# A longer ring for the converted w_in, partly in the place of the second batch's x, and a new set of planner shifts

## The chip, the core and the metric

The kernel runs on one core of a Trainium2 chip. The metric is the device time of one execution in microseconds (us), as the median of several runs. A profiled execution gives the trace that the rows below come from. Engines: PE is the matrix engine (TensorE, PEld its weight loads), DVE is VectorE, ACT is ScalarE, POOL is GpSimd, SP is the queue from which all transfers are issued.

## What is computed

Three stages on 4 batches of 576 tokens, 8 heads of 64, model width 512, in float32 accuracy:

```python
# attention with a decaying causal bias, b = 4, h = 8, s = 576, d = 64
scores = q @ k.T / 8 + min(bias(cumsum(relu(s))), 0), causal
x = softmax(scores) @ v                     # (2304, 512) after joining the heads
h = x @ w_in                                # w_in: 512 x 2048
x2 = (h * cos(h)) @ w_out                   # w_out: 2048 x 512
y = max(x2 @ w1, x2 @ w2, x2 @ w3) @ wo2    # 512 x 768 each, and 768 x 512
```

The weights of the second and third stage come as 64-bit floats.

## The kernel before

**Order of the work.** The kernel is written as a list of operations, each with an engine (or a choice of engines), an estimated duration, a key, and the pieces of memory that it reads and writes. A planner (`Plan`, L45 to L245) works out from the order in the list who must wait for whom, and then lays the operations out in time: each engine takes, of the operations that are ready by the planner's estimates, the one with the smallest key. The order per engine that comes out is fixed in the program. An operation with a choice of engines is offered to the later ones in its list only after a delay (`FLEX`, us by engine). The keys are a step number times 3 plus a shift from tables: `Q_AT`, `K_AT`, `V_AT` for the loads and conversions of q, k and v, `W_AT` for w_in, `S_AT`, `Z_AT`, `T_AT` for the scores, the products with v and the transposes of a step, `O_AT` for w_out. Where the plan leaves PE idle in the first 150 us, it is given matmuls on a constant tile whose result nobody reads (L1538, "fillers" below), and after that none.

**Attention** goes in 32 steps `st`: for each batch b, two ranges r of queries (256 and 320), four pairs p of heads. A step makes its scores (PE, L718 and L722), takes minimum and exponential (DVE L731, ACT L737), splits the weights into two float16 halves (ACT or POOL L412/L416, DVE L442), turns them by a DMA transpose (L754), multiplies with v (PE, L784, all steps in bank 4) and writes x as two float16 halves (ACT L797, DVE L802).

**w_in** comes in 16 chunks of 512 KB through two raw buffers. A chunk c is put from 64 bits into float32 by three DVE operations (L459, L462, L465), into a buffer of the ring `win_b`; its maximum is found on ACT (L477). When four chunks (a group) are there, their common power of two is made (DVE, and PE at L501), and the four are split into float16 halves: `hi` on ACT (L412), or for the fourth on POOL first (L416), and `lo` on DVE (L442) or POOL (L427). Only then can `mm1` (PE, L933) use them. The key of chunk c is `19.5 + 0.29 * c + W_AT[c]`, that of the group's split is the key of its last chunk. `mm1(t)` multiplies the x of a block t (a batch and a range, four steps) with all 16 chunks.

**Where things lie.** `wo_b` is the place of the later w_out, 16 buffers of 2 KB per partition, and is free for other things before:

```python
rb = wo_b[j]                                        # v of the first batch, piece j = 0..4 (L814)
vraw_b = wo_b[5:10]                                 # v of the other batches
win_b = wo_b[0:5] + [wo_b[10]] + stage_b            # ring of 8 for the converted w_in
x_other = [Buf(nc, wo_b[11].lo, 4096).ring(NPAIR),  # x of the second batch: steps 8 to 11 in
           Buf(nc, wo_b[13].lo, 5120).ring(NPAIR)]  # wo_b[11:13], steps 12 to 15 in wo_b[13:16]
value, sp = value_of(words, 512, rb.span(), take("win", win_b), key)     # chunk c (L1049)
```

So chunks 0 to 4 go into the buffers that hold pieces 0 to 4 of the first batch's v, and each can be written only when its piece has been split (`v_split`, L890). The order in which DVE, ACT, POOL and PE then work is in the tables alone.

**After attention** come the gate with `mm` by w_out (PE L1293), and the third stage in seven-product form (PE L1433, L1345); w_out is converted during the last steps of attention.

Of the kernel before, what the change touches and what calls it, by code (L numbers as in the profile page):

```python
# [287 lines left out]
def u_keys(i):  # L288
    return min(128 * (i + 1), S)
# [6 lines left out]
def dve1(n):  # L296
    return 0.07 + 0.00104 * n
# [35 lines left out]
def attn_moe_kernel(ctx, tc, qT, kT, v, s, w_in, w_out, w1, w2, w3, wo2, out):  # L333
# [11 lines left out]
    def alloc(size):  # L345
        b = Buf(nc, used[0], size)
        used[0] += size
        assert used[0] <= ARENA, used[0]
        return b
# [4 lines left out]
    def bspan(i, n=1):  # L354
        return ("ps", Plan.CELL * i, Plan.CELL * (i + n))
# [5 lines left out]
    stage_b = alloc(4096).ring(2)  # L361
    wo_b = alloc(NC1 * 2048).ring(NC1)
# [28 lines left out]
    dip_b = alloc(256)  # L391
    att1 = used[0]
    vraw_b = wo_b[5:10]
    win_b = wo_b[0:5] + [wo_b[10]] + stage_b
    pp_b = pp_b + raw_o
    x_other = [Buf(nc, wo_b[11].lo, 4096).ring(NPAIR), Buf(nc, wo_b[13].lo, 5120).ring(NPAIR)]
    x_last = [Buf(nc, v_b[4].lo, 4096).ring(NPAIR), Buf(nc, k_ring[1][0].lo, 5120).ring(NPAIR)]
# [5 lines left out]
    def take(name, ring):  # L403
        n = rings.get(name, 0)
        rings[name] = n + 1
        return ring[n % len(ring)]


    def scaled(out, src, by, key, cols, reads, writes, on="ACT DVE POOL", late=None, par=False):
# [9 lines left out]
        names = on.split()  # L419
        return P.flex(key, [(e, every[e][0], every[e][1], (FLEX[e] if late is None else late) * (i > 0)) for i, e in enumerate(names)],  # L420
                      reads, writes)

    def minus(out, a, b, key, cols, reads, writes, on="POOL DVE", late=None):
# [6 lines left out]
        names = on.split()  # L430
        return P.flex(key, [(e, every[e][0], every[e][1], (FLEX[e] if late is None else late) * (i > 0)) for i, e in enumerate(names)],
                      reads, writes)
# [47 lines left out]
    def weight_load(src, cols, raw, key, after=(), late=0):  # L480
        m = load(raw.ap(I64, cols), src, 1024 * cols + late, key, writes=[raw.span(0, 8 * cols)])
        P.after(m, [rows_out, *after])
        return raw.ap(I64, cols).bitcast(I32).rearrange("p (n two) -> p n two", two=2)
# [125 lines left out]
    def load_q(st, key):  # L609
        b, r, p = STEPS[st]  # L610
        q0, n = ((0, 256), (256, 384))[r]
        hb, lb = take("q", q_ring)
        hs, ls = [hb.span(0, 4 * n)], [lb.span(0, 4 * n)]
        raw = lb.ap(F32, n)
        load(raw, qT[b, p, :, q0:q0 + n], 512 * n, key - LEAD, writes=ls)
        if b == 0:
            q_of[st] = (raw, None, ls)
            return
        hi, lo = hb.ap(F32R, n), lb.ap(F32R, n)
        scaled(hi, raw, 1.0, key, n, ls, hs, on=Q_ON)  # L620
        minus(lo, raw, r_(hi), key + 0.2, n, ls + hs, ls, on=QS_ON)
        q_of[st] = (hi, lo, hs + ls)

    def load_k(b, p, key):
        hb, lb, rb = take("k", k_ring)
        hs, ls, rs = ([z.span()] for z in (hb, lb, rb))
        raw = lb.ap(F32, S)
        load(raw, kT[b, p], 295e3, key - LEAD, writes=ls, issue=0.65)
        if b == 0 and p == 0:
            row = rb.ap(F32, S)  # L630
            for c0, c1 in ((0, 320), (320, S)):
                first_row(c0, c1, row, [rb.span(4 * c0, 4 * (c1 - c0))], -30 if c0 == 0 else F2_KEY)
            ones = one_b.ap(F32, 128)
            bias = [(ones[64 * h:64 * h + 64], row[64 * h:64 * h + 64]) for h in range(2)]
            bias.append((onef_b.ap(F32, 128), row))
            rs = [rb.span(), one_b.span(), onef_b.span()]
        else:
            row, ones = rb.ap(F32R, S), oner_b.ap(F32R, 128)
            gb = take("got", got_b)
            got, gs = gb.ap(F32, S), [gb.span()]  # L640
            for h in range(2):
                load(got[64 * h:64 * h + 2], rows_dram[b * H + 2 * p + h], 4608, key - RLEAD,
                     reads=[dspan("rows"), dspan("rows", 1)], writes=gs)
            scaled(row, got, 1.0, key, S, gs, rs, on=K_ON)
# [19 lines left out]
    def attention(st):  # L664
# [11 lines left out]
        for i in units:  # L676
            n = u_keys(i)
            tg = 3 * st + i - units[0] + S_AT[st]
            a = 128 * (i - units[0])
# [81 lines left out]
        for j in range(nj):  # L761
# [27 lines left out]

            P.add("PE", 0.05 + 0.16 * max(nu, 0) + 0.1 * r + 0.25 * (j == 0), 3 * st + 2 + Z_AT[st], values,  # L790
                  reads=[ptb.span(), v_of[b, j][1].span()], writes=[bspan(4)])
# [7 lines left out]
            ("DVE", dve1(nq), lambda: nc.vector.tensor_scalar(  # L799
                out=xh, in0=xps, scalar1=us, scalar2=None, op0=ALU.mult), FLEX["DVE"])],  # L800
            reads=[bspan(4)], writes=xh_s)
# [100 lines left out]
    def evac(out, src, key, cols, reads, writes, by=None, on="ACT DVE"):  # L902
# [5 lines left out]
        }  # L908
        P.flex(key, [(e, every[e][0], every[e][1], FLEX[e] * (i > 0)) for i, e in enumerate(on.split())],
               reads, writes)  # L910
# [38 lines left out]
    def out_weights():  # L949
        ws = ws_b.ap(F32, NC1)  # L950
        for c in range(NC1):
            key = WO_KEY + c + O_AT[c]
            rb = take("ro", raw_all)
# [63 lines left out]
    for p in range(NPAIR):  # L1017
        load_k(0, p, -9 if p == 0 else 3 * p - K0 + K_AT[p])
        if p == 0:
            load_q(0, -4)  # L1020
    v_max(0, VM_KEY + V_AT[0])
    v_scale(0, VM_KEY + V_AT[0])
    for j in range(5):
        v_split(0, j, VS_KEY + V_AT[1 + j])
    staged = []
    for st in range(len(STEPS)):
        b, r, p = STEPS[st]
        if st + 1 < len(STEPS):
            load_q(st + 1, 3 * st + Q0 + Q_AT[st])
        if r == 0 and p == 1 and b > 0:  # L1030
            for j in (2, 3, 4):
                v_split(b, j, 3 * st + 1 + V_AT[6 * b + 1 + j])
        attention(st)
        if r == 1 and b + 1 < B:
            load_k(b + 1, p, 3 * st + (6 if p else 3) + K_AT[4 * b + 4 + p])
            if p == 0:
                v_max(b + 1, 3 * st + 1 + V_AT[6 * b + 6])
            if p == 1:
                v_scale(b + 1, 3 * st + 1 + V_AT[6 * b + 6])
            if p == 3:  # L1040
                for j in range(2):
                    v_split(b + 1, j, 3 * st + 1 + V_AT[6 * b + 7 + j])
        if st in WI_AT:
            i_ = WI_AT.index(st)
            for c in range(NC1 * i_ // len(WI_AT), NC1 * (i_ + 1) // len(WI_AT)):
                rb = take("rw", raw_all)
                key = WI_KEY0 + WI_KEY * c + W_AT[c]
                words = weight_load(w_in[c], 512, rb, key - WLEAD)
# [492 lines left out]
    with tc.manual_schedule():  # L1541
# [4 lines left out]
WI_KEY = 0.29  # L1546
WI_AT = (4, 5, 6)
BESIDE = 8
FLEX = {'ACT': 0.19, 'DVE': 2.52, 'POOL': 2.58}
RANK = 0  # L1550
TAIL_LATE = 400e3
PL_POOL = [0, 7, 2]
# [22 lines left out]
FILL_FROM = 1.6  # L1575
FILL = 1.0
SUM_LATE = 20.0
Q_AT = [14.35, 20.56, 2.38, 32.32, -2.23, 3.03, 4.06, 13.13, 14.58, 17.59, 23.87, 46.41, 130.72, 139.71, -11.05,
        -0.13, -0.2, 71.14, -0.24, 133.48, -0.73, -20.41, 0.29, -14.13, -35.27, -13.86, -32.07, 0.89, -1.06, -4.47,
        0, 7.54]  # L1580
K_AT = [-4.84, -0.5, -3.09, -1.11, -2.32, 3.48, 5.41, 23.11, 62.4, -21.8, -24.28, -23.54, 7.02, 141.23, -18.31,
        -6.18]
V_AT = [-0.91, -3.32, -1.76, 1.84, 0.04, 7.09, 2.14, 9.74, 0, -4.17, 4.89, -3.34, 37.96, 3.7, 2.14, 0.16, 5.46, 8.26,
        123.04, 14.3, 2.04, -4.86, -9.16, -0.44]
W_AT = [38.5, 15.22, -0.47, -2.99, 3.9, 28.48, 9.34, -64.41, 1.61, 3.07, 19.94, -15.91, -2.39, -1.32, -18.5, -24.15]
S_AT = [-0.78, -2.47, -0.5, 17.27, -0.41, 1.92, 2.67, -75.63, -50.36, -4.1, 4.26, -5.22, -2.12, -3.3, -13.61, -29.06,
        -21.23, -6.14, 7.23, 0, 2.75, 13.51, 45.86, -2.17, 3.61, 0.44, -3.02, -1.53, -6.53, 1.82, -29.95, 1.75]
Z_AT = [4.67, -12.86, -1.59, -0.47, -1.91, 4.06, -3.51, -0.15, 22.14, 32.92, 4.64, 10.31, 0, -0.78, 8.97, -2.1, 4.28,
        -7.13, -0.46, -13.49, -23.34, -6.6, -21.84, -10.4, 9.01, 3.55, -35.06, -5.75, 11.4, -9.08, 22.09, 10.52]
T_AT = [4.93, 8.19, -14.87, -5.7, -9.82, -7.96, 0.07, -0.29, -14.06, -2.02, 89.71, 1.46, -16.57, 1.97, 55.57, -0.95,  # L1590
        1.81, -4.28, -2.45, 10.96, -15.83, -3.19, -19.02, -3.14, -2.13, 2.5, 0.64, -3.87, 16.77, 0, 1.45, 16.64]
O_AT = [-12.29, 2.91, 0, 25.81, 4.19, 1.49, 0, -0.86, 24.07, 1.14, -3.91, 4.49, -12.23, -3.43, -0.68, -0.11]
FILL_TO = 150.0
FILL_LATE = 0.9
MEM_KEY = [32.0, -4.7, 21.7, 18.9, 25.1, -53.9, -67.3, -36.6, 12.0]
# [79 lines left out]
```

## Time and profile before

| | |
|---|---|
| median of 3 runs | 812.6 us (810.05 to 813.13) |
| the profiled execution | 811.46 us; its span from first to last instruction 809.8 us |
| PE busy in the span | 791.1 us (98%), fillers among it |
| DVE busy | 720.1 us (89%) |
| ACT busy | 572.6 us (71%) |
| POOL busy | 54.8 us (7%) |
| granted PE clock | 0.999 of full |

The span is shorter than the execution by what lies ahead of the first and behind the last instruction. Busy time counts overlapping instructions once, and counts a filler like any other matmul.

### The profile page before, as it was taken

The page shows a single profiled execution, that of the slowest core. Times are in us where ns is not written, and L with a number is a line of the kernel's source. Part 1 is how long each engine was busy: PE and PEld are TensorE (multiplying, and loading weights), DVE is VectorE, ACT ScalarE, POOL GpSimd, SP SyncE. Part 2 cuts the span into 40 slices and gives each one's busy share as a digit, 9 for nine tenths or more (in the row PEclk, how much of TensorE's full clock was granted, in tenths as well). Part 3 has the DMA queues.
Part 4 walks back from the last instruction along what each step waited for, and adds up shares of the span by engine and source line. Part 5 has one row for each costly group of instructions (what it writes and reads, how often), then busy time and mean ns, then how long its engine had stood idle before and what let it go on. Part 6 is the DMA issues. An engine that isn't in the chain of part 4 may idle for free.

```text
span 809.8 us, 17116 instructions
## 1 busy us (share of the span) xinstructions
PE 791.1 (98%) x6283; PEld 533.8 (66%) x6283; DVE 720.1 (89%) x1741; ACT 572.6 (71%) x1250; POOL 54.8 (7%) x83
## 2 busy tenths in 40 slices
PE   8899989999999999999999999999999999999998
PEld 4567877788778867878644444445666666667787
DVE  5899999968996899688999999998999898999683
ACT  3888787988898888769998799954544544554331
POOL 4501122001100100000000010000000000000000
PEclk9999999999999999999999999999999999999999
DMA  7698899989989998966554234303104130000122
GB/s 221 167 221 197 201 253 229 220 197 228 243 195 183 247 188 235 254 219 195 167 156 131 66 105 140 121 0 104 53 1 123 34 105 1 1 1 27 53 79 79
DMA packets 154576, 114.20 MB, mean 141 GB/s; under 512 B 109662, under 2 KB 132446, under 8 KB 154492
## 3 DMA queue, kind: packets, MB, share of 16 engines
q1 hardware_dynamic: 154492, 113.11, 54.5%
q8 instruction: 49, 0.80, 0.4%
q14 instruction: 35, 0.29, 0.1%
HBM read 63.13 MB, written 23.74 MB: 107 GB/s over the span
## 4 chain that ended last, share of the span: by engine, by line
PE 67%; DVE 6%; issue 1%; DMA 1%; POOL 0%; ACT 0%; DVEq 0%; POOLq 0%; SPq 0%
PE banks L1293 23%; PE banks L1433 23%; PE banks L933 10%; PE banks L1345 8%; DVE p L442 2%; PE banks L784 2%; DVE p L731 1%; PE banks L718 1%; DMA p<-in_q_dram 1%; DVE p L977 0%; PE banks L722 0%; DVE p L462 0%; DVE r L425 0%; DVE p L465 0%; DVE p L802 0%
## 5 line engine op out<-in xcount | busy, mean ns | idle before, releaser
L933 PE MATMUL banks<-p,p 128*128 128x256 f16 (+1 forms) x1536 | 199.1, 286 | 1.4 <-ACT p L904 1.4
L1433 PE MATMUL banks<-p,p 128*128 128x384 f16 x1134 | 187.9, 326 | 0.0
L1293 PE MATMUL banks<-p,p 128*128 128x512 f16 (+1 forms) x960 | 187.1, 358 | 0.0
L933 PEld LDWEIGHTS <-p 128*128 128x128 f16 x1536 | 145.8, 98 | 45.1 <-issue 7.4
L442 DVE SCALAR_TENSOR_TENSOR p<-p,p,p 128x512 f16<-128x512 f32 (+4 forms) x244 | 152.0, 649 | 13.7 <-ACT p L412 13.0
L1433 PEld LDWEIGHTS <-p 128*128 128x128 f16 x1134 | 110.8, 98 | 71.0
L412 ACT ACTIVATE p<-p,p 128x512 f16<-128x512 f32 (+4 forms) x242 | 142.0, 624 | 20.9 <-DVE p L745 6.8
L1293 PEld LDWEIGHTS <-p 128*128 128x128 f16 x960 | 93.8, 98 | 92.3
L1443 ACT ACTIVATE p<-banks 128x384 f32<-128x384 f32 x90 | 43.7, 489 | 72.3 <-PE banks L1433 72.3
L904 ACT ACTIVATE p<-banks,p 128x256 f32<-128x256 f32 (+2 forms) x152 | 74.7, 505 | 24.1 <-PE banks L933 21.5
L737 ACT ACTIVATE p<-p,p 128x128 f32<-128x128 f32 (+4 forms) x144 | 82.8, 576 | 5.3 <-DVE p L731 2.3
L731 DVE CUSTOM_DVE_ANT_0 p<-banks,p 128x128 f32<-128x128 f32 (+4 forms) x144 | 71.8, 511 | 2.3 <-POOL p L427 0.4
L514 DVE SCALAR_TENSOR_TENSOR p<-p,p,p 128x512 f16<-128x512 f32 (+2 forms) x73 | 61.8, 866 | 6.4 <-ACT p L511 6.4
L1345 PE MATMUL banks<-p,p 128*128 128x256 f16 x567 | 65.3, 273 | 0.0
L511 ACT ACTIVATE p<-p,p 128x512 f16<-128x512 f32 (+2 forms) x73 | 56.1, 810 | 12.9 <-DVE p L1136 9.2
L1345 PEld LDWEIGHTS <-p 128*128 128x128 f16 x567 | 55.5, 98 | 8.7
L1279 ACT ACTIVATE p<-p,p 128x512 f32<-128x512 f32 (+1 forms) x80 | 51.4, 669 | 12.4 <-DVE p L1276 12.4
L477 ACT ACTIVATE p<-p 128x512 f16<-128x512 f32 x61 | 38.2, 626 | 21.7 <-DVE p L465 17.6
L1538 PE MATMUL banks<-p 128*128 128x384 bf16 (+1 forms) x321 | 49.4, 306 | 2.6 <-POOL p L576 1.1
L1282 DVE TENSOR_TENSOR p<-p,p 128x512 f32<-128x512 f32 (+1 forms) x80 | 49.1, 635 | 2.9 <-ACT p L1279 2.6
L718 PE MATMUL banks<-r,r 64*128 64x256 f32 (+3 forms) x360 | 48.1, 340 | 3.1 <-DVE p L731 1.7
L1460 DVE TENSOR_TENSOR p<-banks,p 128x384 f32<-128x384 f32 x81 | 44.1, 550 | 6.8 <-PE banks L1433 6.1
(97 smaller groups left out, 877.7 us busy)
## 6 DMA issues: line engine op xcount, KB each, us to landing
p<-h_dram SPq DMA_DIRECT2D x64, 256.0 KB
p<-in_moe_w_out_dram SPq DMA_DIRECT2D x22, 512.0 KB
h_dram<-p SPq DMA_DIRECT2D x32, 320.0 KB
p<-in_moe_w_dram SPq DMA_DIRECT2D x18, 512.0 KB
p<-in_moe_w_in_dram SPq DMA_DIRECT2D x16, 512.0 KB
h_dram<-p SPq DMA_DIRECT2D x32, 256.0 KB
p<-in_k_dram SPq DMA_DIRECT2D x16, 288.0 KB
out_dram<-p SPq DMA_DIRECT2D x17, 256.0 KB
```

What stands on the lines that cost most here:

```text
L412: "ACT": (slow(cols, 0.19 if par else 0.09), lambda: nc.scalar.activation(out=out, in_=src, func=AF.Copy, scale=by)),
L442: n = P.add("DVEP", dve1(cols) + 0.06, key, lambda: nc.vector.scalar_tensor_tensor(out=lo, in0=src, scalar=by, in1=hi, op0=ALU.mult, op1=A ...
L511: P.add("ACT", slow(cols), key, lambda: nc.scalar.activation(out=hi, in_=src_, func=AF.Copy, scale=by), reads=reads, writes=hi_sp)
L514: P.add("DVEP", dve1(cols) + 0.06, key, lambda: nc.vector.scalar_tensor_tensor(out=lo, in0=src_, scalar=by, in1=hr, op0=ALU.mult, op1=ALU. ...
L718: nc.tensor.matmul(sp[:, o:o + kn], qq[rows_of[h], at:at + 128], kk[rows_of[h], k0:k0 + kn], start=(m == 0 and bool(opens)), stop=False)
L731: nc.vector.tensor_tensor_reduce(out=e, in0=sc, in1=km, op0=ALU.add, op1=ALU.min, scale=-0.125, scalar=3.0e38, accum_out=mn[:, j:j + 1]),
L737: "ACT", act(n, 0.28), tg, lambda j=j, e=e, mn=mn, sm=sm: nc.scalar.activation(out=e, in_=e, func=AF.Exp, scale=-1.0, bias=mn[:, j:j + 1], ...
L904: "ACT": (act(cols, 0.05 if by is None else 0.15), lambda: nc.scalar.activation(out=out, in_=src, func=AF.Copy, scale=1.0 if by is None el ...
L933: nc.tensor.matmul(hp, w[:, wp, ks], xx, start=(k == 0 and m == 0), stop=(k == KD - 1 and m == 2),)
L1293: nc.tensor.matmul(bank(base + d)[:, 0:n], w[:, wp, ds], xx, start=(c == 0 and z == 0), stop=(c == NC1 - 1 and z == 2))
L1345: nc.tensor.matmul(o, h[hp], w[wp], start=(opens and f == 0 and m == 0), stop=(closes and f == 2 and m == 2), skip_group_check=True)
L1433: nc.tensor.matmul(bank(z)[:, 0:TB], w_, x_, start=(opens and j == 0 and k == 0), stop=(j == 1 and k == 2), skip_group_check=True)
```

## The change

The ring of the converted w_in gets four more buffers at its front, `wo_b[11:15]`. Chunks 0 to 3 go there, chunks 4 to 8 into `wo_b[0:5]`, chunk 9 into `wo_b[10]`, 10 and 11 into `stage_b`, and 12 to 15 into `wo_b[11:15]` again. These four buffers are also where the x of the second batch is written from step 8 on; so step 8's x now has to come after the split of chunk 12, and step 10's after that of chunk 13. Then the three `FLEX` delays and the eight tables of shifts are replaced. No operation is added or taken away.

```diff
-    win_b = wo_b[0:5] + [wo_b[10]] + stage_b
+    win_b = wo_b[11:15] + wo_b[0:5] + [wo_b[10]] + stage_b
...
-FLEX = {'ACT': 0.19, 'DVE': 2.52, 'POOL': 2.58}
+FLEX = {'ACT': 5.55, 'DVE': 2.21, 'POOL': 2.09}
...
-W_AT = [38.5, 15.22, -0.47, -2.99, 3.9, 28.48, 9.34, -64.41, 1.61, 3.07, 19.94, -15.91, -2.39, -1.32, -18.5, -24.15]
+W_AT = [-0.11, -5.94, 12.54, 32.59, -11.48, 33.93, 2.98, -47.92, 2.66, -10.08, 9.52, 0, 6.85, -0.48, -51.84, -52.17]
```

`Q_AT`, `K_AT`, `V_AT`, `S_AT`, `Z_AT`, `T_AT` and `O_AT` are replaced in the same way, every number of them.

## Rows read from the trace of the kernel before

**Rows 1.** The profile's page: span, and busy time by engine
```profile
span 809.8 us, 17116 instructions
PE 791.1 (98%) x6283; PEld 533.8 (66%) x6283; DVE 720.1 (89%) x1741; ACT 572.6 (71%) x1250; POOL 54.8 (7%) x83
```

**Rows 2.** Stretches: length, busy us (instructions) by engine, clock, DMA share, GB/s
```profile
0.00:61.00 61.00, 53.38 (x405) 34.32 (x405) 50.23 (x162) 42.11 (x116) 21.88 (x44) 1.00 0.79 203
61.00:113.00 52.00, 46.69 (x583) 38.61 (x580) 50.33 (x152) 43.20 (x113) 8.23 (x10) 1.00 0.91 215
113.00:160.00 47.00, 45.81 (x420) 34.31 (x419) 46.53 (x137) 40.72 (x97) 10.53 (x11) 1.00 0.95 225
...
400.00:700.00 300.00, 300.00 (x1609) 156.99 (x1608) 286.26 (x540) 203.07 (x362) 2.55 (x2) 1.00 0.26 80
```

**Rows 3.** Stretches, fillers (L1538) alone: length, PE busy, PEld busy
```profile
0.00:61.00 61.00, 34.20 (x180) 17.70 (x180) 1.00 0.79 203
61.00:113.00 52.00, 15.21 (x141) 11.83 (x141) 1.00 0.91 215
73.00:93.00 20.00, 9.07 (x89) 7.31 (x89) 1.00 0.99 228
```

**Rows 4.** Timeline of SP: the first v and w_in transfers are issued
```profile
10.31 1.78 SPq L450 DMA_DIRECT2D p<-in_v_dram  x4
13.70 0.90 SPq L450 DMA_DIRECT2D p<-in_moe_w_in_dram  x2
```

**Rows 5.** Stretches of 2 us, all engines, columns as in rows 2
```profile
18.00:20.00 2.00, 1.45 (x12) 1.01 (x13) 0.73 (x4) 2.00 (x6) 0.82 (x2) 1.00 0.67 272
20.00:22.00 2.00, 2.00 (x15) 1.21 (x13) 0.94 (x6) 1.94 (x8) 0.48 (x1) 1.00 0.48 87
```

**Rows 6.** Timeline of DVE: start, us, operation, [idle before it]
```profile
25.80 0.97 DVE L442 SCALAR_TENSOR_TENSOR p<-p,p,p 128x512 f16<-128x512 f32 x1 [0.22 <-ACT p L412]
...
26.96 0.65 DVE L459 TENSOR_SCALAR p<-p 128x512 int32<-128x512 int32 x1
...
38.69 0.69 DVE L465 SCALAR_TENSOR_TENSOR p<-p,p 128x512 int32<-128x512 int32 x1
```

**Rows 7.** The stretch from 18.3 to 26.9 us, all engines, columns as in rows 2
```profile
18.30:26.90 8.60, 7.72 (x60) 4.97 (x61) 5.41 (x25) 8.53 (x27) 3.33 (x5) 1.00 0.61 166
```

**Rows 8.** Groups by line: busy us, mean ns of one, idle before
```profile
L1293 PE MATMUL banks<-p,p 128*128 128x512 f16 (+1 forms) x960 | 187.1, 358 | 0.0
L462 DVE SCALAR_TENSOR_TENSOR p<-p,p 128x512 int32<-128x512 int32 x56 | 38.7, 692 | 0.4
L465 DVE SCALAR_TENSOR_TENSOR p<-p,p 128x512 int32<-128x512 int32 x56 | 38.5, 689 | 0.4
L459 DVE TENSOR_SCALAR p<-p 128x512 int32<-128x512 int32 x56 | 23.5, 422 | 6.4 <-DMA p<-in_moe_w_out_dram 3.4 <-DMA p<-in_moe_w_dram 3.0
```

**Rows 9.** Timeline of PE: powers of w_in's groups (L501), mm1 (L933)
```profile
55.88 0.22 PE L501 MATMUL banks<-p,p 128*128 128x128 bf16 x1 [0.67 <-DVE p L498]
...
61.09 1.48 PE L933 MATMUL banks<-p,p 128*128 128x256 f16 x12
...
89.59 0.22 PE L501 MATMUL banks<-p,p 128*128 128x128 bf16 x1 [0.21 <-DVE p L498]
...
130.93 0.23 PE L501 MATMUL banks<-p,p 128*128 128x128 bf16 x1
...
168.55 1.49 PE L933 MATMUL banks<-p,p 128*128 128x256 f16 x12
```

**Rows 10.** Timeline of DVE: x of steps 3, 8, 11 (L802), last split of w_in
```profile
51.77 0.42 DVE L802 SCALAR_TENSOR_TENSOR p<-banks,p 128x256 f16<-128x256 f32 x1
...
108.69 0.40 DVE L802 SCALAR_TENSOR_TENSOR p<-banks,p 128x256 f16<-128x256 f32 x1
...
139.01 1.40 DVE L442 SCALAR_TENSOR_TENSOR p<-p,p,p 128x512 f16<-128x512 f32 x2
140.34 0.41 DVE L802 SCALAR_TENSOR_TENSOR p<-banks,p 128x256 f16<-128x256 f32 x1
```

More of the change, by code (lines that the diff above doesn't have):

```diff
@@ L1577 @@
 SUM_LATE = 20.0
[L1578 to L1584, printed above, removed]
@@ L1585 @@
-W_AT = [38.5, 15.22, -0.47, -2.99, 3.9, 28.48, 9.34, -64.41, 1.61, 3.07, 19.94, -15.91, -2.39, -1.32, -18.5, -24.15]
[L1586 to L1589, printed above, removed]
@@ L1590 @@
-T_AT = [4.93, 8.19, -14.87, -5.7, -9.82, -7.96, 0.07, -0.29, -14.06, -2.02, 89.71, 1.46, -16.57, 1.97, 55.57, -0.95,
-        1.81, -4.28, -2.45, 10.96, -15.83, -3.19, -19.02, -3.14, -2.13, 2.5, 0.64, -3.87, 16.77, 0, 1.45, 16.64]
-O_AT = [-12.29, 2.91, 0, 25.81, 4.19, 1.49, 0, -0.86, 24.07, 1.14, -3.91, 4.49, -12.23, -3.43, -0.68, -0.11]
+Q_AT = [-0.42, -3.17, -0.15, -0.99, 14.15, -39.12, -2.68, 110.06, 2.55, 14.16, 32.04, 114.48, 172.81, 0.77, -0.54,
+        -1.14, -45.5, -0.61, -1.35, -8.35, 0.16, 7.26, -9.76, 9.93, -36.18, 3.34, -6.43, 4.55, 8.37, -4.49, -1.76,
+        0.01]
@@ new lines @@
+K_AT = [-0.35, 0.88, -4.24, -3.13, -1.43, -2.73, 0.79, 43.28, 41.94, -10.24, -3.26, 1.8, 16.1, -0.33, -0.45, 11.54]
+V_AT = [-1.14, 1.46, -4.47, -1, 10.34, -22.18, 3.82, 3.25, 6.36, 14.69, -1.3, 52.84, 36.28, -44.54, 0, -6.51, 3.31,
+        0.7, 202.2, -7.12, 12.63, -5.84, 2.49, 47.58]
+W_AT = [-0.11, -5.94, 12.54, 32.59, -11.48, 33.93, 2.98, -47.92, 2.66, -10.08, 9.52, 0, 6.85, -0.48, -51.84, -52.17]
+S_AT = [-2.96, -5.89, 2.12, 19.41, -1.01, -3.4, 12.77, -98.46, -39.56, 10.11, 25.38, -2.04, 0, -25.77, -1.07, 11.63,
+        -1.21, 1.68, 2.72, -3.18, -2.59, -50.26, 3.87, 35.07, -3.48, -0.8, 6.85, -5.56, 1.31, -30.17, 0.56, 16.22]
@@ new lines @@
+Z_AT = [4.6, -5.8, -3.88, 1.79, -7.58, -1.07, 0.27, -9.53, -0.54, -0.69, 0.42, 6.67, -1.37, -0.96, -10.2, -8.05,
+        -4.36, -1.19, -2.97, 19.01, -0.8, -9.27, -13.08, -11.17, 18.16, -3.69, 20.96, 11.84, -5.72, -1.2, 1, -2.08]
+T_AT = [7.4, -3.8, 0.52, -7.37, 1.39, 5.55, -16.03, 1.75, -57.68, -1.36, 55.89, 0.04, 2.39, -5.26, -2.55, 23.58, 0,
+        4.19, -18.49, 0, 4.53, 0.37, 1.52, 0.71, -1.35, 3.4, 14.15, -6.69, 0, -3.65, 32.71, -6.08]
+O_AT = [-7.15, 18.19, 8.7, 24.59, 0, 6.74, 0, -24.96, -14.98, 23.9, -0.54, -7.69, -34.48, -18.95, -4.81, -18.87]
```

## The prediction

> **What bounds the kernel now.** I read the page first. PE is busy 791.1 of 809.8 us [rows 1], which looks like a kernel that only fewer matmuls could shorten. But PE's time holds fillers, so the second view is the stretches, once for all engines and once for the fillers. Up to 61 us PE has 34.20 us of fillers and is idle for 61.00 - 53.38 = 7.62; from 61 to 113 it has 15.21 us of fillers and 52.00 - 46.69 = 5.31 idle [rows 2, 3]. After 113 there are no fillers, and the idle time that is left of the whole is 809.8 - 791.1 - 7.62 - 5.31 = 5.8 us. So PE is starved for 41.8 + 20.5 = 62.3 us at the beginning, and from 113 us on it is the bound: whatever is to be won must let PE do more of its real work before 113.
>
> What starves it is DVE. From 61 to 113 DVE is busy 50.33 of 52.00, and from 113 to 160 46.53 of 47.00 [rows 2]. In the first 61 us it has 10.77 us to spare, and a good part of these lies just ahead of the first conversion of w_in, the place that the change touches. So the third view is the timeline there. The transfers of the first two chunks are issued at 13.70, behind those of v [rows 4]. The queue moves 272 GB/s until 20 us and 87 GB/s after that [rows 5], so I take them to have landed by about 20 us, the first perhaps 2 us sooner. The first operation on a chunk starts at 26.96, straight behind the L442 of 25.80 that splits a 128x512 piece of v, and the second chunk is through only at 38.69 + 0.69 = 39.4 [rows 6]. No row shows DVE waiting for v at 26.96: the order of the instructions was made for that wait. From 18.3 to 26.9 DVE is busy 5.41 of 8.60 us, so 3.19 us lie idle while two chunks are in their raw buffers [rows 7].
>
> **The change part by part.** No instruction is added or removed, and the same bytes are moved, so what counts is where the instructions of the early phase come to stand.
>
> The ring. Chunks 0 and 1 need L459, L462 and L465: 0.422 + 0.692 + 0.689 = 1.80 us each, 3.6 for both [rows 8]. Freed from v, they fit nearly into the 3.19 us that DVE has between 18.3 and 26.9. That time is lost to the DVE queue today, since behind it DVE is full until 160 us. DVE work drawn into it brings all that follows on DVE forward by as much, and with it the moment from which PE has enough to do. That is worth time one for one, because behind it only PE's own work is left. I take 3 us, the end that the idle row gives: the conversions need nothing of ACT, which is full there with 8.53 of 8.60 us. The bounds are 0 (the gaps are pieces below 2 us in a chain between ACT and DVE, and a conversion of 0.69 in a gap of 0.3 delays what the gap was waiting for) and 3.6 (both chunks vanish from later). Chunks 2 and 3 are freed too, but their raw buffers come free only behind chunks 0 and 1, and their transfers follow; a gain of theirs is the next term's.
>
> At 26.96 L459 took 0.65 us, with POOL at work, where the mean of the 56 is 0.42 [rows 6, 8]. POOL is busy 3.33 of the 8.60 us [rows 7], so some of the six operations may be slower there; for two L459 that is 0.46 us less of gain, which stays inside the bounds.
>
> The order. The tables decide in which order DVE works off conversions and attention steps. Groups come slowly now: the powers stand at 55.88 and 89.59, the last at 130.93 [rows 9]. From the first to the second are 33.7 us, though four chunks cost DVE 4 x (1.80 + 0.70) = 10.0 us with their `lo`, of which two take 1.40 us [rows 8, 10]. In that wait PE has 9.07 us of fillers from 73 to 93 [rows 3]. Four chunks give one block 4 x 1.48 = 5.9 us of real work [rows 9], so a second group that came ten or more us sooner could replace 5.9 us of fillers. The upper bound of this term is therefore 6 us for one group, and twice that if the following groups move too. The new `W_AT` doesn't point one way: eight chunks get a smaller key and eight a larger one, and the split of a group goes by its last chunk, whose shift grows by 35.6, 16.5 and 15.9 for the first three groups and falls by 28.0 for the last. A later split of the early groups would cost as much as an earlier one gives, so the lower bound is -4. Between -4 and 6 I take 2.5, nearer to the gain, because the ring lets the first group be complete earlier whatever the key of its split, while x of the first block, written by 51.77 + 0.42 = 52.2, is not what mm1 waits for at 61.09 [rows 9, 10].
>
> The other tables and `FLEX`. The larger delay for ACT touches operations that name ACT second or later, that is q's rounding (POOL first). It can only move such work from ACT to POOL, which has 54.8 us of work in 809.8 [rows 1]. I take 0, with 1 us either way: in the early phase POOL's 21.88 of 61 us cover it [rows 2], and without that cover the price would be the wait of one step's scores. The later tables order a phase in which PE has 1.2 us idle from 113 to 160 and none from 400 to 700 [rows 2]; there is nothing in it to win and, with PE full, little to lose, 0.
>
> Sum: 3 + 2.5 + 0 = 5.5 us. The profiled execution took 811.46, 1.7 above its span and 1.1 below the median of the runs, so I take the difference to the median: 812.6 - 5.5 = 807.1.
>
> **The rivals.** *Nothing comes of it.* ACT is full from 18.3 to 26.9 [rows 7] and each chunk still needs its pass there before the power. If what paces the early phase is the chain through ACT and not DVE's sum of work, conversions in DVE's gaps only empty later slots, and PE starts mm1 no sooner. Against it speaks that DVE is the fuller one from 61 to 160. Time 812, between 810 and 814.
>
> *Slower: step 8's x waits for w_in.* x of step 8 now lies where chunk 12 is, and that is free only when the last group is split. Before, that x is written at 108.69 and the last split ends at 139.01 + 1.40 = 140.4; x of step 11 ends 32 us after that of step 8 began, at 140.75, and mm1 first needs that block's x at 168.55 [rows 9, 10]. So the last split may move no later than 168.55 - 32 = 136.5 unless the steps behind it come faster. If it stays at 140.4, PE runs dry by 3.9 us; if conversions are pushed behind attention by another 5 us, by 9. That gives 816.5 to 821. All products with v go through one bank, so the products of steps 9 to 11 queue behind the late x. Against it: with all conversions done by then, the four steps should take less than 32 us, since DVE has no conversions between them.
>
> *Nothing, by another way: the seam.* From 400 to 700 DVE is busy 286.26 of 300 us [rows 2]. If DVE paced that part, PE's earlier arrival would be given back there. Against it: no idle time of PE in the whole stretch, and none ahead of any of the 960 matmuls of L1293 [rows 2, 8]. Time 812.6. The Trainium skill (Perfetto Trace Analysis, Identifying the Most-Contended Engine) holds that matmul busy time is no fair measure of TensorE's distance from its limit, and that weight loads' busy share should be read in its place, with occupancy for VectorE. By that rule 156.99 of 300 us would leave PE far from full and DVE would be the contended engine there; the trace's idle rows speak against it as far as they go, so I give the seam only a small chance.
>
> *Much faster.* If the new order completes all four groups before step 8's x, as it must to keep that x on time, PE could lose half of its 20.5 us of starvation between 61 and 113: 812.6 - 10 - 3 = about 800.
>
> **How the numbers follow.** About 0.5%, 4 us, is what a measurement can tell from no change here, so faster begins below 808.5. Chances: the forecast 0.50, with a range of its own of 803.5 to 809.5, of which 0.05 lies above 808.5; nothing by way of ACT 0.22; the seam 0.05; much faster 0.08; the wait for x 0.15. Faster is 0.45 + 0.08 = 0.53, the same 0.05 + 0.22 + 0.05 = 0.32, slower 0.15. The range leaves out the far side of the much faster case below 800 and part of the slow case above 816; it takes in the bounds of both terms, 812.6 - 3.6 - 6 - 1 = 802 and 812.6 + 4 - 0 = 816.6 nearly.
>
> **What the new profile would show.** If the ring's term is right, the first L459 stands near 20 us instead of 26.96, DVE's busy time between 18.3 and 26.9 is about 8 instead of 5.41 us, and the first mm1 is 3 us or more ahead of 61.09. If the order's term is right, the second power stands well ahead of 89.59 and the fillers from 61 to 113 are fewer than 15.21. PE's real work, 791.1 - 49.4 = 741.7 us, must be the same, so that the difference of the spans is that of fillers and idle time. The prediction is wrong on the slow side if ACT or DVE shows a wait that ends with the split of a w_in chunk ahead of L797 or L802 near 109 us, with fillers or idle PE behind it. It is wrong in its reason if DVE fills its early gaps and the fillers of 61 to 113 stay.

## The result, and the profile after

The changed kernel took 816.32 us (median of 5 runs, 813.99 to 818.19); beside it on the same chip the kernel before took 811.26 (5 runs, 809.57 to 813.13). The ratio is 1.007, with a 95% interval of 1.0051 to 1.0089. It is slower by 0.7%, just above the top of the predicted range and on the other side of no change. The profiled execution has a span of 814.6 us, against 809.8 [rows 1], so 4.8 us are to be found.

The page, span and busy time by engine, of the kernel after:

```profile
span 814.6 us, 17137 instructions
...
PE 794.9 (98%) x6292; PEld 535.6 (66%) x6292; DVE 722.0 (89%) x1741; ACT 572.5 (70%) x1249; POOL 58.7 (7%) x84
```

The stretches of the kernel after, all engines (columns as in rows 2):

```profile
0.00:61.00 61.00, 54.21 (x400) 34.73 (x401) 52.35 (x163) 41.09 (x113) 23.69 (x44) 1.00 0.85 212
61.00:113.00 52.00, 45.97 (x560) 37.18 (x558) 50.08 (x149) 41.34 (x103) 7.02 (x9) 1.00 0.98 195
113.00:160.00 47.00, 46.06 (x410) 34.47 (x410) 43.91 (x139) 43.45 (x112) 8.18 (x10) 1.00 0.86 220
160.00:400.00 240.00, 239.07 (x2475) 189.02 (x2468) 201.50 (x602) 197.79 (x494) 14.83 (x20) 1.00 0.89 215
400.00:700.00 300.00, 298.26 (x1593) 155.32 (x1592) 284.44 (x535) 204.79 (x364) 4.97 (x2) 1.00 0.27 81
...
18.30:26.90 8.60, 7.40 (x55) 4.51 (x52) 7.04 (x27) 7.49 (x25) 2.60 (x5) 1.00 1.01 205
```

And its fillers alone:

```profile
0.00:61.00 61.00, 34.35 (x187) 18.31 (x188) 1.00 0.85 212
61.00:113.00 52.00, 16.80 (x142) 11.97 (x139) 1.00 0.98 195
113.00:160.00 47.00, 0.41 (x3) 0.28 (x3) 1.00 0.86 220
```

Fillers and idle time together are the time in which PE is starved: 34.35 + 61.00 - 54.21 = 41.1 us up to 61 (before 41.8), 16.80 + 52.00 - 45.97 = 22.8 from 61 to 113 (before 20.5) and 1.35 from there to 160 (before 1.2): 65.3 instead of 63.5. From 400 to 700 PE, full before [rows 2], now lacks 1.74 us. So the loss has two places, one early and one long after attention. The DVE column tells what became of the head start. By 61 us DVE has done 52.35 - 50.23 = 2.1 us more than before; by 113 it is 1.9 more, and by 160 it is 0.75 less, since from 113 to 160 it was busy 43.91 instead of 46.53 [rows 2]. A second pair of profiles, of the two kernels that differ from these only behind 437 us (the cut of L1148 below), shows a lead of 0.1 us at 61 and a lag of 1.9 at 160. So the lead is no larger than what two executions differ by, and in both pairs it is gone before 160.

Timeline of DVE, kernel after (start, us, operation, [idle before it]): the first conversions, x of step 3, the `lo` splits of the first group among the L442 rows, and x of step 8:

```profile
20.37 0.43 DVE L459 TENSOR_SCALAR p<-p 128x512 int32<-128x512 int32 x1 [1.37 <-DMA p<-in_moe_w_in_dram]
...
23.36 0.69 DVE L465 SCALAR_TENSOR_TENSOR p<-p,p 128x512 int32<-128x512 int32 x1
...
53.35 0.42 DVE L802 SCALAR_TENSOR_TENSOR p<-banks,p 128x256 f16<-128x256 f32 x1
...
64.04 0.74 DVE L442 SCALAR_TENSOR_TENSOR p<-p,p,p 128x512 f16<-128x512 f32 x1
...
68.91 1.47 DVE L442 SCALAR_TENSOR_TENSOR p<-p,p,p 128x512 f16<-128x512 f32 x2
...
134.31 0.42 DVE L802 SCALAR_TENSOR_TENSOR p<-banks,p 128x256 f16<-128x256 f32 x1
...
553.63 2.26 DVE L442 SCALAR_TENSOR_TENSOR p<-p,p,p 128x512 f16<-128x512 f32 x3
```

Timeline of PE, kernel after: the powers, the first `mm1`, the end of attention, and the end of the second stage:

```profile
50.82 0.23 PE L501 MATMUL banks<-p,p 128*128 128x128 bf16 x1
...
70.08 1.48 PE L933 MATMUL banks<-p,p 128*128 128x256 f16 x12
...
90.22 0.22 PE L501 MATMUL banks<-p,p 128*128 128x128 bf16 x1
...
110.98 1.70 PE L784 MATMUL banks<-p,p 128*64 128x64 f16 x52 [0.85 <-DMA p<-p]
...
375.50 4.75 PE L1293 MATMUL banks<-p,p 128*128 128x256 f16 x42
...
553.27 0.38 PE L1293 MATMUL banks<-p,p 128*128 128x512 f16 x1 [0.95 <-ACT p L412]
554.43 10.30 PE L1293 MATMUL banks<-p,p 128*128 128x512 f16 x47 [0.79 <-DVE p L442]
564.57 1.63 PE L1433 MATMUL banks<-p,p 128*128 128x384 f16 x9
```

The first two chunks are converted from 20.37 to 24.0 instead of 26.96 to 39.4 [rows 6], and the first power comes 5 us sooner, at 50.82 instead of 55.88. Yet the first `mm1` comes 9 us later, at 70.08 instead of 61.09 [rows 9]: the `lo` splits of that group stand at 64.04 to 70.3. For the place of the loss, the marks are those at which PE turns from one stage to the next, here and in the timeline of the kernel before:

```profile
373.02 3.22 PE L1293 MATMUL banks<-p,p 128*128 128x256 f16 x28
...
559.91 2.28 PE L1433 MATMUL banks<-p,p 128*128 128x384 f16 x13
```

Attention ends 2.5 us later (375.50 against 373.02), the second stage takes 189.1 instead of 186.9 us, 2.2 more, and from there to the end it is 250.0 against 249.9. So 4.8 = 2.5 + 2.2 + 0.1. Up to the end of attention PE has 51.56 us of fillers and 14.69 of idle time (before 49.41 and 15.35), which makes 1.5 of the 2.5 us. The other 1.0 is the matmuls' own time: PE's busy time without fillers, which the prediction held to be fixed, is 794.9 - 51.6 = 743.3 us instead of 741.7, and of these 1.6 us 1.0 lie ahead of 375.50 and 0.45 in the second stage. In the second pair of profiles attention ends 2.5 us later too, by 2.2 us of fillers and idle time and 0.3 of matmuls.

### The profile page after: what moved, and what is told of

Read it like the earlier page. It is cut to its first block, busy times and chain, and to the rows that moved or that the text cites. A ratio compares the mean times of both kernels' runs of the same rounds, so it can differ in the third digit from the quotient of the medians.

```text
span 814.6 us, 17137 instructions
## 1 busy us (share of the span) xinstructions
PE 794.9 (98%) x6292; PEld 535.6 (66%) x6292; DVE 722.0 (89%) x1741; ACT 572.5 (70%) x1249; POOL 58.7 (7%) x84
## 4 chain that ended last, share of the span: by engine, by line
PE 53%; DVE 15%; ACT 3%; DMA 2%; issue 1%; SPq 0%; ACTq 0%; DVEq 0%
PE banks L1433 23%; PE banks L933 11%; PE banks L1293 8%; PE banks L1345 8%; DVE p L442 4%; DVE p L514 3%; DVE p L1276 2%; DVE p L1282 2%; PE banks L718 2%; DVE p L1136 1%; PE banks L784 1%; DVE p L731 1%; ACT p L412 1%; DMA p<-in_moe_w_out_dram 1%; DMA p<-p 1%
## 5 line engine op out<-in xcount | busy, mean ns | idle before, releaser
L933 PE MATMUL banks<-p,p 128*128 128x256 f16 (+1 forms) x1536 | 199.0, 286 | 0.4 <-ACT p L904 0.3
L1293 PE MATMUL banks<-p,p 128*128 128x512 f16 (+1 forms) x960 | 187.5, 358 | 1.7 <-ACT p L412 0.9
L933 PEld LDWEIGHTS <-p 128*128 128x128 f16 x1536 | 145.8, 98 | 43.3 <-issue 5.2
L442 DVE SCALAR_TENSOR_TENSOR p<-p,p,p 128x512 f16<-128x512 f32 (+4 forms) x244 | 155.7, 664 | 15.5 <-ACT p L412 14.7
L412 ACT ACTIVATE p<-p,p 128x512 f16<-128x512 f32 (+4 forms) x243 | 142.9, 624 | 25.9 <-DVE p L1282 6.3
L1293 PEld LDWEIGHTS <-p 128*128 128x128 f16 x960 | 93.8, 98 | 94.4 <-issue 2.5
L737 ACT ACTIVATE p<-p,p 128x256 f32<-128x256 f32 (+4 forms) x144 | 82.8, 576 | 10.0 <-DVE p L731 6.3
L511 ACT ACTIVATE p<-p,p 128x512 f16<-128x512 f32 (+3 forms) x73 | 56.2, 808 | 15.5 <-DVE p L1136 8.9
L514 DVE SCALAR_TENSOR_TENSOR p<-p,p,p 128x512 f16<-128x512 f32 (+3 forms) x73 | 61.6, 872 | 3.9 <-ACT p L511 3.9
L1538 PE MATMUL banks<-p 128*128 128x384 bf16 (+1 forms) x330 | 51.6, 309 | 3.7 <-DVE p L802 1.5
L477 ACT ACTIVATE p<-p 128x512 f16<-128x512 f32 x61 | 38.0, 623 | 20.5 <-DVE p L465 17.5
L718 PE MATMUL banks<-r,r 64*128 64x256 f32 (+3 forms) x360 | 47.7, 340 | 2.0 <-DVE p L731 1.7
```

Of the source, the lines that this page charges most:

```text
L412: "ACT": (slow(cols, 0.19 if par else 0.09), lambda: nc.scalar.activation(out=out, in_=src, func=AF.Copy, scale=by)),
L442: n = P.add("DVEP", dve1(cols) + 0.06, key, lambda: nc.vector.scalar_tensor_tensor(out=lo, in0=src, scalar=by, in1=hi, op0=ALU.mult, op1=A ...
L514: P.add("DVEP", dve1(cols) + 0.06, key, lambda: nc.vector.scalar_tensor_tensor(out=lo, in0=src_, scalar=by, in1=hr, op0=ALU.mult, op1=ALU. ...
L718: nc.tensor.matmul(sp[:, o:o + kn], qq[rows_of[h], at:at + 128], kk[rows_of[h], k0:k0 + kn], start=(m == 0 and bool(opens)), stop=False)
L737: "ACT", act(n, 0.28), tg, lambda j=j, e=e, mn=mn, sm=sm: nc.scalar.activation(out=e, in_=e, func=AF.Exp, scale=-1.0, bias=mn[:, j:j + 1], ...
L933: nc.tensor.matmul(hp, w[:, wp, ks], xx, start=(k == 0 and m == 0), stop=(k == KD - 1 and m == 2),)
```

## The experiments

Two kinds were run. In the first the tables, delays or buffers are changed, so that the planner lays out another order. In the second the order stays, instruction by instruction, and only some instructions are made narrower or some fillers are left out. The narrower kernels leave out a part of the work, so they only show what time is worth at a place.

**The two halves of the change.** Ring alone, in the kernel before:

```diff
-    win_b = wo_b[0:5] + [wo_b[10]] + stage_b
+    win_b = wo_b[11:15] + wo_b[0:5] + [wo_b[10]] + stage_b
```

> The kernel before with the longer ring alone, old tables and FLEX. Theory 1 (the new tables lose the time, the ring gives 0 to 3 us): 808 to 811.5 us, the first L459 near 20 us. Theory 2 (the ring loses it, because step 8's x must wait for w_in): 814 us or more, step 8's x behind the last w_in split, later than 130 us, and more fillers and idle PE time than 68 us in all.

Measured: 827.21 us, ratio to before 1.0186 (1.0164 to 1.0209); the profile is of the slowest of six executions, 830.51. The powers and the first `mm1` come far earlier, as the ring promises, but x of step 3 falls back from 51.77 [rows 10] to 67.20. Timeline of PE, then of DVE, ring alone:

```profile
44.24 0.22 PE L501 MATMUL banks<-p,p 128*128 128x128 bf16 x1
...
49.61 0.82 PE L933 MATMUL banks<-p,p 128*128 128x256 f16 x6
...
360.81 0.30 PE L784 MATMUL banks<-p,p 128*64 128x256 f16 x2
364.46 3.04 PE L784 MATMUL banks<-p,p 128*64 128x64 f16 x52 [3.35 <-DMA p<-p]
```

```profile
67.20 0.41 DVE L802 SCALAR_TENSOR_TENSOR p<-banks,p 128x256 f16<-128x256 f32 x1
```

So an `mm1` that starts 11.5 us sooner went with a kernel that is 15.6 us slower. The freed conversions overtake the attention steps. Up to 160 us starvation is 73.4 us (before 63.5), and at the end of attention PE waits for the transpose of a late step. x of step 8 stands at 131.71, as the second theory expects, but only 2.9 us behind that of step 7: it is late because the steps ahead of it are. Tables and `FLEX` alone, that is the kernel after with the old ring:

```diff
-    win_b = wo_b[11:15] + wo_b[0:5] + [wo_b[10]] + stage_b
+    win_b = wo_b[0:5] + [wo_b[10]] + stage_b
```

> The kernel before with the new tables and FLEX alone, ring of 8. Theory 1 (tables): 815 to 820 us, as slow as the changed kernel or up to 3 us slower for want of the ring, first mm1 near 70 us. Theory 2 (ring): 811 to 813 us.

Measured: 826.3 us, 1.0186 (1.016 to 1.0212), which neither theory has; the first `mm1` comes at 84.4, and PE is idle for 7.4 us from 160 to 400 (before 1.2). Each half costs 1.9%, and both together 0.7%: the parts of this change don't add up.

**The late first group and FLEX.** In the kernel after, the shift of the first group's last chunk, or the three delays, are set back:

```diff
-W_AT = [-0.11, -5.94, 12.54, 32.59, -11.48, ...
+W_AT = [-0.11, -5.94, 12.54, -2.99, -11.48, ...
```

> The changed kernel with one number back, the shift of chunk 3, which is also the key of the first group's split (32.59 to -2.99). If the late split of the first group is what starves PE from 53 to 70 us: first mm1 near 60 us instead of 70.1, fillers from 60 to 80 us down by 3 to 6 us, and the time 811 to 814. If that starvation is only moved to where the next group is awaited: first mm1 earlier, the sum of fillers and idle time unchanged within 1 us, 815 to 817.

```diff
-FLEX = {'ACT': 5.55, 'DVE': 2.21, 'POOL': 2.09}
+FLEX = {'ACT': 0.19, 'DVE': 2.52, 'POOL': 2.58}
```

> The changed kernel with the old FLEX delays. If FLEX takes no part, as the prediction has it: 815 to 818, no more than 1 us from the changed kernel. If the later ACT choice for q's rounding, or the earlier DVE and POOL choices, lose time: below 814.

Measured: 826.54 us, 1.0189 (1.0162 to 1.0215), and 830.75 us, 1.0234 (1.021 to 1.0259). With the earlier key the first `mm1` moved only from 70.08 to 66.4, the first power fell back from 50.82 to 59.8, and the time grew by 10 us: 3.9 us more starvation up to 160, and 6.3 more idle time from there to 400. The new order loses in other places, so this run can't tell what the late first group costs. With the old `FLEX` the early phase has 65.4 us of starvation, as in the kernel after; the loss lies at the end of attention. Timelines of PE there, first for the earlier key, then for the old `FLEX`:

```profile
360.12 3.04 PE L784 MATMUL banks<-p,p 128*64 128x64 f16 x52 [5.41 <-DMA p<-p]
```

```profile
363.37 3.04 PE L784 MATMUL banks<-p,p 128*64 128x64 f16 x52 [7.57 <-DMA p<-p]
```

In both the transpose of a last step comes 5 to 8 us too late, and PE has nothing else left to do. The new `FLEX` in the kernel before:

```diff
-FLEX = {'ACT': 0.19, 'DVE': 2.52, 'POOL': 2.58}
+FLEX = {'ACT': 5.55, 'DVE': 2.21, 'POOL': 2.09}
```

> The kernel before with the three new FLEX delays alone. If FLEX is of no weight by itself, as the prediction had it: 810 to 812.5. If the tables and FLEX are fitted to each other, so that any one of them alone upsets the order: 813 us or more, with PE waiting for a transpose or for x near the end of attention, 340 to 375 us.

Measured: 817.87 us, 1.0084 (1.0065 to 1.0102). Only some five instructions change their engine (ACT has 1245 instead of 1250), yet PE's idle time from 160 to 400 grows from 1.2 to 4.9 us, 3.5 of it in waits of the scores (L718) for DVE and none for a transpose. Three delays that were costed at nothing move the time by 0.8% in one set of tables and by 1.6% in the other.

**What DVE time is worth in the early phase.** In the kernel before, with its order kept, two of the three conversions of chunks 0 to 3 work on 64 of 512 columns, and the other columns are left half converted:

```diff
-            out=bits, in0=high, scalar=-0x40000000, in1=bits, ...
+            out=bits[:, :n], in0=high[:, :n], scalar=-0x40000000, in1=bits[:, :n], ...
...
-            out=bits, in0=low, scalar=29, in1=bits, ...
+            out=bits[:, :n], in0=low[:, :n], scalar=29, in1=bits[:, :n], ...
...
-... take("win", win_b), key)
+... take("win", win_b), key, 64 if c < 4 else None)
```

> The kernel before, every instruction in the same place and order, but L462 and L465 of w_in's chunks 0 to 3 work on 64 of 512 columns (these chunks' values are then not w_in's). DVE has some 4.5 us less to do before 50 us. Theory 1 (a DVE head start in the early phase is worth time one for one, as the prediction took it): 806 to 808 us. Theory 2 (the order on PE, with its fixed number of fillers, paces the early phase, and a head start of DVE is waited away): 810.5 to 813 us, DVE's idle time ahead of 113 us longer by 3 to 4.5 us and the fillers unchanged at 49 us.

Measured: 809.86 us beside 810.56, ratio 0.9992 (0.9977 to 1.0006). By the page DVE has 720.1 - 716.7 = 3.4 us less to do; the eight instructions still took 0.21 us each. The time fell by about 0.7 us, by the interval between 1.9 us less and 0.5 more, so it lies between the two expectations and can't be told from nothing; one for one, 3.4 us, is excluded. Where the rest went is seen in the stretch that follows the cuts, in the kernel before and in this one:

```profile
35.00:61.00 26.00, 23.84 (x186) 16.16 (x186) 25.79 (x85) 22.31 (x59) 2.85 (x5) 1.00 0.89 204
```

```profile
35.00:61.00 26.00, 24.68 (x195) 16.83 (x192) 22.99 (x81) 21.97 (x59) 2.68 (x3) 1.00 0.94 211
```

DVE was full, 25.79 of 26.00 us, with no wait. Relieved, it stands idle for 3.0 us, and its waits in this stretch are 1.6 us for ACT's L797, 0.9 for ACT's L737 and 0.5 for ACT's L412. PE's idle time falls from 2.16 to 1.32 us, its fillers up to 61 us stay (34.38). The next two take off a part of the fillers, with and without the cut:

```diff
-FILL = 1.0
+FILL = 0.75
...
-FILL_LATE = 0.9
+FILL_LATE = 0.6
```

> The same with a quarter of the early fillers and a third of the late ones left out (FILL 0.75, FILL_LATE 0.6). If the fillers hold PE back where DVE is early: 805 to 809 us. If DVE's chain paces PE whatever it is fed: as the kernel with the same fewer fillers and whole conversions, within 1.5 us.

> The kernel before with fewer fillers alone. If fillers only fill what is idle anyway: 810.5 to 813, with the idle time up by what the fillers lose. If they hold PE back: below 809. If PE's granted clock falls behind the gaps: above 814 and rows with a clock below 1.0.

Measured: with the cut 811.65 us, 1.0007 (0.9993 to 1.0021); without it 812.93, 1.0027 (1.0015 to 1.004). Fewer fillers are slower in themselves (more on this below). With them fewer the cut is worth 0.0020 of the ratio, 1.6 us, which the intervals don't tell from 0.7; its own interval is 0.1 to 3.1 us. So this pair doesn't settle how much of the head start the fillers swallow: PE must work through them in its fixed order, and in the cuts here they stay, so that only idle time of PE can be won. The same cut further on, in chunks 4 to 7 of both kernels, and in all 16 of the kernel before:

```diff
+... take("win", win_b), key, 64 if 4 <= c < 8 else None)
...
+... take("win", win_b), key, 64)
```

> The kernel before, same order, with L462 and L465 of chunks 4 to 7 on 64 of 512 columns (their values are then not w_in's): DVE has some 4.5 us less to do between 54 and 90 us, where it is full. If DVE paces PE there: 806 to 807.5, with idle and filler time of PE between 61 and 113 us down by 3 us or more. If the head start is waited away as the one before 50 us was: 809.5 to 811.

> The same cut in the changed kernel, where the conversions of chunks 4 to 6 stand ahead of the first group's split. If DVE's late split is what keeps the first mm1 at 70 us and costs the 2 us: first mm1 near 66, 812 to 813.5. If PE's order and its fillers hold it: first mm1 still near 69 to 70 and 815 to 817.

> The kernel before, same order, with the cut in all 16 chunks: some 19 us less for DVE before 126 us. The ceiling of what DVE's time is worth in this order. If one for one: near 792 us, as far as PE's 13 us of early idle time go, 798. If PE's own order with its fillers is the pace: 807 or more.

Measured: 0.9977 (0.9962 to 0.9993) in the kernel before, that is 1.9 us for 3.7 us of DVE time; 1.0047 (1.0028 to 1.0065) in the kernel after, against its 1.007; and 0.9954 (0.9939 to 0.997), 3.7 us, for all chunks, where the page shows 720.1 - 706.4 = 13.7 us less DVE time. In the kernel after this is a step of 1.9 us, give or take 2.2, and the first `mm1` stands at 67.3 instead of 70.08, with 1.2 us of that already in the first conversion; so that run leaves both of its theories open. Page lines of the first and the last of the three:

```profile
PE 788.8 (98%) x6283; PEld 533.5 (66%) x6283; DVE 716.4 (89%) x1741; ACT 572.1 (71%) x1250; POOL 52.2 (6%) x83
```

```profile
PE 790.6 (98%) x6283; PEld 535.1 (66%) x6283; DVE 706.4 (88%) x1741; ACT 571.5 (71%) x1250; POOL 55.4 (7%) x83
```

With the order kept, a microsecond of DVE time was worth 0.2 us ahead of the first group (the interval allows 0 to 0.55), 0.5 in the second (0.15 to 0.83) and 0.27 over all four (0.18 to 0.36). In the last the fillers stay at 49.1 us, and PE's idle time up to 113 falls from 12.9 to 9.5: nearly all that was won came out of idle time.

**The end of the second stage.** In both kernels, order kept, L1148, which looks for a maximum, reads 64 of 768 columns, which takes work from DVE in the stretch from 400 us on:

```diff
-                out=small.ap(F32, 8)[:, i:i + 1], in_=x2_b[tp].ap(F32, 2 * TB, 8 * TB * i), op=ALU.max,
+                out=small.ap(F32, 8)[:, i:i + 1], in_=x2_b[tp].ap(F32, 64, 8 * TB * i), op=ALU.max,
```

> The changed kernel, same order, but the twelve reductions of L1148 read 64 of 768 columns (the common power then comes from a part of x2). Eight of them lie ahead of 550 us and give DVE some 5 us. If the 1.7 us that PE is idle near 553 us are DVE's arrears at the end of the second stage: no idle time of L1293 and 813.5 to 815. If something else holds ACT and DVE there, such as a transfer: 816 or more, idle time as before.

> The control for the shortened reductions: the kernel before, same order, L1148 on 64 of 768 columns. If the second stage of the changed kernel is held by arrears of DVE that the kernel before doesn't have: 810 to 812.5, no change beyond 0.15%. If DVE's work there costs both kernels: 807 to 809, the gain of the changed kernel's cut.

Measured: the kernel after falls to 813.0 us, ratio to before 1.0024 (1.001 to 1.0037) instead of 1.007; the kernel before stays as it is, 0.9993 (0.9979 to 1.0006). Stretch and timeline of PE, kernel after with the cut:

```profile
400.00:700.00 300.00, 300.00 (x1606) 156.62 (x1604) 278.23 (x540) 206.08 (x365) 4.96 (x2) 1.00 0.27 81
```

```profile
562.33 3.90 PE L1433 MATMUL banks<-p,p 128*128 128x384 f16 x23
```

The 1.74 us of idle time are gone, the third stage begins at 562.33 instead of 564.57, and in the kernel before, which has no idle time there, 8.0 us less DVE work (720.1 to 712.1) bring nothing. The piece is 2.2 us by the timeline and 0.46% by the two ratios, 3.7 us give or take 1.9 (half-widths 0.0019 and 0.0014, as a root of squares 0.0023).

**The wait of step 8's x.** In the kernel after, chunks 12 to 15 get `wo_b[0:4]`, so that the x of the second batch waits for no split:

```diff
-    win_b = wo_b[11:15] + wo_b[0:5] + [wo_b[10]] + stage_b
+    win_b = wo_b[11:15] + wo_b[0:5] + [wo_b[10]] + stage_b + wo_b[0:4]
```

> The changed kernel with chunks 12 to 15 in wo_b[0:4] instead of wo_b[11:15]: the first four chunks still do not wait for v, but step 8's x need no longer wait for the last split of w_in, only for the first group's. If that wait costs the changed kernel its time: step 8's x near 115 us instead of 134, and 811 to 814. If it costs nothing because PE has the first two blocks to work on until about 165 us: 815.5 to 818.

Measured: 815.86 us, ratio to before 1.0063 (1.0044 to 1.0081), by the intervals the same as the kernel after. Timeline of DVE, x of steps 8 and 9:

```profile
116.45 0.41 DVE L802 SCALAR_TENSOR_TENSOR p<-banks,p 128x256 f16<-128x256 f32 x1
...
124.47 0.42 DVE L802 SCALAR_TENSOR_TENSOR p<-banks,p 128x256 f16<-128x256 f32 x1
```

The x that stood at 134.31 comes 18 us sooner, and nothing is won that could be told from noise. The order is another one here too, but the kernel after says the same: from 113 to 160 its PE is busy 46.06 of 47.00 us, with 0.41 us of fillers, so it has other work while that x is awaited.

## Why the prediction was wrong, by its steps

**The ring.** The conversions did move: L459 starts at 20.37, and DVE is busy 7.04 instead of 5.41 us between 18.3 and 26.9 (about 8 was forecast). That is 1.6 of the 3 us: DVE waits 1.37 us until 20.37 for the first chunk's transfer, so the part of the idle row ahead of it was not free for these conversions. The step that failed is the one behind it, that a head start of DVE is "worth time one for one, because behind it only PE's own work is left". DVE was full, but the fixed orders of ACT, PE and DVE are interlocked: spared 3.4 us, DVE ran into waits for ACT of 3.0 us within the same 26 us, and some 0.2 of each microsecond reached the end. By that price the ring's 3 us would have been 0.6, and at most 1.7 by the interval. In the kernel after not even that is seen, as what lead DVE had at 61 is a lag at 160. The prediction's own sign of being wrong in its reason came out: DVE fills its early gaps, and the fillers of 61 to 113 stay (16.80 against 15.21 us). The rival "nothing comes of it" named the chain through ACT and fits this step better than the forecast did; how much of the head start that chain holds back, and how much the fillers in PE's order, stays open.

**The order.** The term was +2.5 of gain and came out with the other sign. The text saw that the first group's key grows by 35.6 and set it aside, "because the ring lets the first group be complete earlier whatever the key of its split". The power did come earlier, the split did not: 64.04 to 70.3, and the first `mm1` at 70.08. The second power, which was to stand well ahead of 89.59, stands at 90.22. From 61 to 113 starvation grew by 2.3 us (2.5 in the second pair of profiles); with what is won and lost in the rest of attention, 1.5 to 2.2 us of the 2.5 by which it ends later are starvation. But setting the key of the group back doesn't mend it (that order is 10 us slower), nor is an early group the measure (49.61 in the ring alone, 827 us). It is the whole order that loses there; which of the shifts does it stays open.

**Other tables and FLEX.** "0, with 1 us either way" was wrong by its reason too. The text asked which operations `FLEX` names, and how much work it moves. The planner takes each operation in the light of what it placed before, so a few moved choices change the order of all that follows: the delays alone cost 0.84% in the kernel before. "Nothing in it to win and, with PE full, little to lose" overlooked that PE is full from 160 on only as long as the last steps' transposes are in time; three of the orders tried here lost 3 to 8 us in one wait at that point. With the new delays in the kernel before it was another wait, that of the scores for DVE.

**The rivals.** The late x did come (134.31 instead of 108.69) and cost nothing that shows: PE is starved for only 1.35 us from 113 to 160, and the early release won nothing. The seam, at 0.05 the least of them and forecast as no change, was one of the two pieces, 2.2 of 4.8 us by the timelines, 3.7 give or take 1.9 by the ratios. Stretches from PE's first matmul of the second stage to DVE's last splits for L1293, all engines, kernel before and kernel after, and those splits in the timeline of DVE, kernel before:

```profile
373.02:548.66 175.64, 175.64 (x913) 88.95 (x911) 173.99 (x303) 154.47 (x272) 2.55 (x2) 1.00 0.38 114
```

```profile
375.50:553.63 178.13, 177.18 (x918) 89.51 (x916) 176.20 (x310) 155.44 (x275) 4.97 (x2) 1.00 0.39 115
```

```profile
548.66 2.07 DVE L442 SCALAR_TENSOR_TENSOR p<-p,p,p 128x512 f16<-128x512 f32 x3
```

DVE is busy for 99% of both. In the kernel after it still has 310 instructions to do when PE enters the stage, before 303: 2.2 us more, the amount by which the stage is longer. Against PE the splits come 178.13 - 175.64 = 2.5 us later, and PE waits for 1.74 of these; with the cut of L1148 they come 175.69 us behind that matmul, and PE has no wait. The prediction read PE's idle rows of the kernel before, which were zero, as distance from this bound; by these rows the slack behind them was under 1 us (an estimate). Where in attention DVE falls behind stays open. By 400 us it has done 351.27 us of work before and 347.84 after, and from 113 to 400 it waited for ACT's L412 for 9.0 us before and 12.8 after. But with the early release of x it has done 350.92 by 400, and PE has the same two waits near 553 (1.17 and 0.79 us), behind 310 instructions of DVE again. The Trainium skill (Perfetto Trace Analysis, Identifying the Most-Contended Engine) takes occupancy as a fair measure of how close VectorE is to its limit, and the 99% agree that DVE was at its limit there. That DVE set the time is shown only for the kernel after: with 8 us less of its work the kernel before did not move.

The sum, by the timelines: 2.5 us lost up to the end of attention and 2.2 at the end of the second stage, where a gain of 5.5 and no change had been forecast. No order tried here beat the kernel before; the kernels below it in time leave out work. Whether the longer ring pays with other tables stays open.

## What to carry to other kernels

Where the order on every engine is fixed, don't price a head start of one engine at its full length, however busy that engine is: keep the order, make a few of its instructions narrower, and measure what a microsecond of it is worth at that place (here 0.27 over all four groups, with an interval of 0.18 to 0.36). Where a planner makes one order out of shifts, delays and buffers together, these have no parts to be costed one by one: five single steps between the two versions (the ring put in or taken out, the delays put in or taken out, one shift) each cost 0.8 to 1.9% beside the version they started from. For stages with no idle time on the bound engine, look for how far the second engine lies ahead of its deadline, not only for idle rows: here 2.2 us more of DVE work at the start of a stage came due 178 us later.

## What was not expected of the hardware

After a wait of several us PE ran its next matmuls at half the clock. The group of 52 matmuls at L784 takes 1.70 us at 110.98 in the kernel after, behind a wait of 0.85 us, and 3.04 behind waits of 3.35, 5.41 and 7.57. Stretches of the kernel after with the old `FLEX`:

```profile
350.00:363.00 13.00, 4.75 (x77) 3.59 (x75) 2.10 (x4) 1.57 (x3) 0.00 (x0) 0.84 0.74 198
363.00:366.40 3.40, 3.03 (x53) 2.96 (x53) 1.02 (x2) 0.00 (x0) 0.00 (x0) 0.50 0.33 96
366.40:372.00 5.60, 5.60 (x33) 3.50 (x33) 2.18 (x6) 5.22 (x12) 0.00 (x0) 0.75 0.53 177
```

The granted clock is 0.50 of full, 1.2 GHz, while they run, and is still below full on the mean until 372. Ahead of 363 PE had been busy 4.75 of 13.00 us. So such a wait costs more than its length, here 3.04 - 1.70 = 1.3 us more for these 52 matmuls alone.

Whether fillers keep the clock up is less plain. Stretches of the kernel before with fewer fillers, then of the one with fewer fillers and the cut in chunks 0 to 3:

```profile
0.00:61.00 61.00, 46.25 (x336) 29.74 (x338) 47.31 (x152) 39.96 (x112) 20.42 (x42) 0.97 0.84 190
61.00:113.00 52.00, 42.77 (x534) 34.72 (x533) 50.33 (x155) 44.05 (x113) 9.61 (x12) 0.98 0.99 213
```

```profile
0.00:61.00 61.00, 49.38 (x375) 31.82 (x376) 48.55 (x164) 44.37 (x121) 23.90 (x45) 1.00 0.86 209
61.00:113.00 52.00, 42.63 (x538) 34.51 (x537) 50.06 (x157) 43.15 (x112) 7.02 (x10) 1.00 0.95 213
```

Both have about a quarter less filler time up to 61 us (25.72 and 26.59 us instead of 34.20) and a third less from there to 113, and only one shows a lower clock; it is the slowest of its twelve executions. Two kernels with all their fillers show 0.97 in one of these stretches as well: the kernel after with the cut of L1148 up to 61 us, the kernel before with all chunks cut from 61 to 113. Over all executions the mean granted clock was 0.9966 with fewer fillers and 0.9985 in the kernel before, and with the cut 0.9981 and 0.9995. So it falls in some executions of each of these kernels, on the mean further with fewer fillers, and the kernel with fewer fillers was 0.27% slower; that the clock alone makes these 0.27% is not shown.
